# A gated block behind low-rank attention on one core: the gate by x-times-sigmoid, scores in pairs

## The chip, the cores and the metric

One NeuronCore of a Trainium2 chip runs the whole program; the other cores are idle. The metric is the time of one execution on the device in microseconds (us). TensorE (PE) multiplies matrices into PSUM, with its weight loads shown as an engine of their own (PEld). VectorE (DVE) and ScalarE (ACT) can read PSUM, GpSimd (POOL) works on SBUF alone here, and SyncE (SP) issues transfers.

## The reference

Eight batches of eight heads, 1024 positions, 64 columns per head. Keys and values are first projected along the sequence to 64 rows, then ordinary softmax attention is computed over those 64, the heads are put side by side, and a gated feed-forward block follows:

```python
k_proj = einsum('ks,bhsd->bhkd', E, k)
v_proj = einsum('ks,bhsd->bhkd', F, v)
scores = (q @ k_proj.T) / sqrt(64)          # per batch and head
attn   = softmax(scores)                    # over the 64 projected rows
x      = heads side by side(attn @ v_proj)  # 8192 x 512
g      = x @ w_gate                         # 8192 x 1536
silu   = g * (1 / (1 + exp(-g)))
out    = (silu * (x @ w_val)) @ w_out       # 8192 x 512
```

## The kernel before

Tokens are worked in 16 chunks of 512, two to each batch; `c` counts chunks and `c = 2b` is the first of batch `b`. A chunk has 12 tiles `f` of 128 hidden columns, so there are 192 tiles `t`. The main loop runs over `t`, and each tile has this order:

```python
f_g(c, f, i)              # gate: 4 matmuls, then ACT
run_slot(2 * t)
f_v(c, f, i)              # value: 4 matmuls, then DVE
for fn, *a in late.pop(t, ()):
    fn(*a)                # output product of the chunk before, half sums
run_slot(2 * t + 1)
```

The order is written out by hand: nothing reorders it, and each engine takes its own instructions in it. `f_g` computes the gate in a bank of the PSUM pool `gps` (two banks), and ACT writes its hyperbolic tangent of half the value to `th` (L534). `f_v` computes the value in `vps` (two banks); DVE makes `(th + 1) * g` from the PSUM gate (L541) and then half of that times the value, `hT` in bf16 (L546). Together these are x-times-sigmoid times value, as `x * sigmoid(x) = x / 2 * (1 + tanh(x / 2))`.

The output product of a chunk is done during the next one. From the second chunk on it has seven products of half size in place of eight (`f_m`, L624), for two row groups: 14 steps `n` per chunk, placed one or two to a tile, six matmuls each. It needs sums of quarters of `hT` (`h_sum`, L607; on POOL for two of them, on DVE for three). Some steps end in copies by ACT (L641 `xs` at steps 1 and 8, which stand in tiles 1 and 7; L648 `ysb` at steps 3 and 10, in tiles 3 and 9) and in sums by DVE and POOL (L643, L653, L654, L659), and then SP stores the rows.

The attention of batch `b` is spread over the tiles of the batch before it in the loop. `place(b)` writes its units into slots, two slots to a tile, counted from `s0 = 48 * (b - 1)`, which is the first tile of chunk `2b - 2`: `u_KV` projects keys and values, `u_KT` turns the keys, `u_TD` turns the queries by DMA on SP's queue. Eight score units `u_S` have 4 matmuls each (L364) into a bank of the pool `a` (two banks), and ACT takes the exponential (L372) into `ee`. `u_R` makes row sums and reciprocals on DVE (L394, L395), `u_N` scales the weights on POOL (L409) and adds to a watched sum (L425). `u_AD` turns the weights by DMA on SP's queue after four units, `u_PVt` multiplies by the values, and ACT copies the result to `xT` (L477). In the kernel before, the eight score units stand at eight different slots, about three slots apart. Loads of the next batch's keys, values and queries are issued on POOL's queue.

After the loop a branch leads to a general path for scores that need their maximum subtracted; the inputs here do not take it.

Of the kernel before, what the change touches and what calls it, by code (L numbers as in the profile page):

```python
# [9 lines left out]
AF = mybir.ActivationFunctionType  # L10
ALU = mybir.AluOpType
AX = mybir.AxisListType
BF16 = mybir.dt.bfloat16
FP32 = mybir.dt.float32

B = 8
# [6 lines left out]
P = 128  # L23
# [3 lines left out]
NFT = DFF // P  # L27
CH = 2
CW = 512
# [3 lines left out]
HC = DM // 2  # L33
HT = CW // 2
ENG = [getattr(mybir.EngineType, n) for n in ("PE", "DVE", "Activation", "SP", "Pool")]
BY_DMA = [(b, ch) for b in range(1, B) for ch in range(CH)]


@with_exitstack
def kernel(  # L40
# [19 lines left out]
    nc = tc.nc  # L60
    scale = 1.0 / float(D) ** 0.5
# [7 lines left out]
    h_pool = ctx.enter_context(tc.tile_pool(name="hT", bufs=2))  # L69
# [27 lines left out]
    kb, vb, qb, xT, hT = {}, {}, {}, {}, {}  # L97
# [50 lines left out]
    maxed = []  # L148
# [160 lines left out]
    qT, ee, rr, AA, AT = {}, {}, {}, {}, {}  # L309
    by_dma = list(BY_DMA)  # L310

# [195 lines left out]
    gp = {}  # L507
# [3 lines left out]
    def f_mm(c, f, w, i=None):  # L511

        if i != 1:


            where = "y" if (c, f, w) == (0, 2, 0) else "gv"[w]
            half[c, f, w] = bank(where, [P, CW], FP32, where + "ps")
        ps = half[c, f, w]
        x = xT[divmod(c, CH)]
        ts = slice(0, CW) if i is None else slice(256 * i, 256 * (i + 1))  # L520
        for kt in range(NKT):
            nc.tensor.matmul(  # L522
                out=ps[:, ts],
                lhsT=(wg, wv)[w][:, kt, f * P : (f + 1) * P],
                rhs=x[:, kt, ts],
                start=(kt == 0),
                stop=(kt == NKT - 1),
            )
        return ps

    def f_g(c, f, i=None):
        ps = f_mm(c, f, 0, i)
        th = fw.tile([P, CW], FP32, name="th", tag="th")
        nc.scalar.activation(out=th[:], in_=ps[:], func=AF.Tanh, scale=0.5)  # L534
        gp[0] = (ps, th)

    def f_v(c, f, i=None):
        ps = f_mm(c, f, 1, i)
        g, th = gp.pop(0)
        s1 = fw.tile([P, CW], FP32, name="s1", tag="s1")  # L540
        nc.vector.scalar_tensor_tensor(  # L541
            out=s1[:], in0=th[:], scalar=1.0, in1=g[:], op0=ALU.add, op1=ALU.mult
        )
        if f == 0:
            hT[c] = h_pool.tile([P, NFT, CW], BF16, name="hT", tag="hT")
        nc.vector.scalar_tensor_tensor(  # L546
            out=hT[c][:, f, :], in0=s1[:], scalar=0.5, in1=ps[:], op0=ALU.mult, op1=ALU.mult
        )
# [173 lines left out]
    def put(s, fn, *a):  # L722
        slots[s].append((fn, a))

    def place(b):
        s0 = 48 * (b - 1)
        if b == 1:
            put(22, u_TD, 1, 0)
            put(29, u_K1, 1)
            put(32, u_KT, 1)  # L730
            put(40, u_V1, 1)
            sa = (35, 36, 37, 38, 41, 42, 43, 44)
            put(41, u_AD, 1, 0)
            put(30, u_TD, 1, 1)
            put(47, u_AD, 1, 1)
            put(46, u_PVt, 1, 0, (0, 1), ("aa", "av"))
        else:
            if b == 2:
                put(s0 + 10, u_KV, b)
            else:  # L740
                put(s0 + 8, u_KV, b, "kv", (0, H), "v")
            put(s0 + (13 if b == 2 else 11), u_KT, b)
            put(s0 + (9 if b == 2 else -6), u_TD, b, 0)
            put(s0 + (11 if b == 2 else -4), u_TD, b, 1)
            sa = [s0 + j for j in ((17, 18, 22, 23, 27, 30, 33, 36) if b == 2 else (14, 17, 20, 23, 26, 29, 32, 35))]
            put(sa[3] + 4, u_AD, b, 0)
            put(sa[7] + 4, u_AD, b, 1)
            put(s0 + 44, u_PVt, b, 0, (0, 1), ("aa", "yz"))
        for j in range(NJ):
            put(sa[j], u_S, b, j)  # L750
            put(sa[j] + 1, u_R, b, j)
            put(sa[j] + 1, u_N, b, j)
        put(s0 + (68 if b == 1 else 56), u_PVt, b, 1, (0, 1), ("aa", "yz"))

    def run_slot(s):
# [14 lines left out]
    def u_bad():  # L770
        bad.append(nc.values_load(flag[:], min_val=0, max_val=1, skip_runtime_bounds_check_because="is_le gives 0 or 1"))
        tc.mark_branch_hint_location("general", hint=bad[0], engines=tuple(ENG))

    def general():
# [6 lines left out]
        with tc.For_i(0, B) as turn, tc.manual_schedule():  # L781
            turn_of.append(turn)
            b = 0
            load_k(b)
            load_v(b)
            u_KV(b)
            u_KT(b)
            for ch in range(CH):
                c = CH * b + ch
                load_q(b, ch)  # L790
                for u in range(4 * ch, 4 * ch + 4):
                    u_T(b, u)
                    u_S(b, u)
                    u_R(b, u)
                    u_N(b, u)
                    u_A(b, u)
                u_PVt(b, ch, (0, 1), ("aa", "yz"))
                for f in range(NFT):
                    f_g(c, f)
                    f_v(c, f)  # L800
                for m in (1, 2, 5, 6, 7):
                    h_sum(c, m, 0, HF, nc.vector)
                for n in range(14):
                    f_m(c, n)

    with tc.manual_schedule():
# [3 lines left out]
        for i in range(2):  # L810
            nc.scalar.dma_start(
                out=kraw[i][:],
                in_=k[0, 2 * i : 2 * i + 2].rearrange("h (p j) d -> p h (j d)", j=NJ),
# [125 lines left out]
        for b in range(1, B):  # L939
            place(b)  # L940
        for b in range(2, B):
            s0 = 48 * (b - 1) - (20 if b == 3 else 24)
            at = (43, 43, 44, 45) if b == 2 else (s0, s0 + 2, s0 + 4, s0 + 6)
# [31 lines left out]
        for t in range(NIT):  # L975
            c, f = divmod(t, NFT)
            ring["wide"] = c < 2
            i = 1 if t < 2 else None
            f_g(c, f, i)
            run_slot(2 * t)  # L980
            f_v(c, f, i)
            for fn, *a in late.pop(t, ()):
                fn(*a)
            run_slot(2 * t + 1)
# [34 lines left out]
```

## Time and profile before

| | us |
|---|---|
| median of 3 runs | 548.73 |
| lowest and highest | 548.31, 549.86 |
| the profiled execution | 548.89 |
| its span | 547.2 |
| PE busy | 536.7 |
| DVE busy | 413.7 |
| ACT busy | 232.8 |
| POOL busy | 305.9 |

The span runs from the first to the last instruction in the profile. In the rows of a timeline the first number is the start, the second the length of the piece, then engine, line, operation, the written tile and what is read, shapes, the number of instructions merged, and in brackets the idle time before with what ended it. A PE matmul's shown end is modelled and overlaps its successor, so PE's rows are read from start to start.

### The profile page before, as it was taken

How to read it: one execution, taken by the hardware profiler on the slowest of the kernel's cores; microseconds unless marked ns; L12 is line 12 of the kernel's file. 1: busy time of each engine (PE TensorE's matmuls, PEld its weight loads, DVE VectorE, ACT ScalarE, POOL GpSimd, SP SyncE). 2: the span in 40 equal slices, each digit the busy share in tenths (PEclk: the TensorE clock that was granted, in tenths of full speed). 3: DMA queues.
4: the chain of work that ended last, by engine and by line, in shares of the span. 5: the costliest groups of instructions: out<-in, count | busy, mean ns of one | idle time of the engine just before them, and what ended most of it. 6: DMA issues, size and time to landing. Idle time of an engine off the chain costs nothing.

```text
span 547.2 us, 9550 instructions
## 1 busy us (share of the span) xinstructions
PE 536.7 (98%) x3558; PEld 313.6 (57%) x3558; DVE 413.7 (76%) x702; ACT 232.8 (43%) x416; POOL 305.9 (56%) x428
## 2 busy tenths in 40 slices
PE   7999999999999999999999999999999999999996
PEld 3654445556556555566555665566555655555665
DVE  3687897779668876779677795687857887676883
ACT  3565453353444434344434444434444443443331
POOL 6962395478616864177632966248661666416171
PEclk9999999999999999999999999999999999999999
DMA  9999969929921599008961199512991123101003
GB/s 194 191 195 200 159 147 198 173 78 161 196 67 41 103 191 207 21 21 155 197 148 39 40 154 204 106 40 64 184 202 54 39 78 78 40 38 40 8 32 120
DMA packets 112227, 62.92 MB, mean 115 GB/s; under 512 B 65968, under 2 KB 103856, under 8 KB 112176
## 3 DMA queue, kind: packets, MB, share of 16 engines
q0 software_dynamic: 43952, 29.49, 37.6%
q1 hardware_dynamic: 67392, 31.46, 26.3%
q10 hardware_dynamic: 832, 1.31, 0.8%
q8 instruction: 29, 0.48, 0.4%
q14 instruction: 22, 0.18, 0.1%
HBM read 60.29 MB, written 16.78 MB: 141 GB/s over the span
## 4 chain that ended last, share of the span: by engine, by line
PE 94%; DMA 4%; ACT 0%; issue 0%; DVE 0%; POOL 0%; DVEq 0%; ACTq 0%; POOLq 0%
PE vps L522 31%; PE gps L522 30%; PE yps L624 25%; PE sc L364 2%; DMA wv<-in_moe_w_val_dram 2%; PE kvp L173 2%; PE yps L558 2%; PE pv L468 1%; DMA qb<-in_q_dram 1%; POOL AA L409 0%; PE kvp L212 0%; PE kvp L197 0%; PE qTp L329 0%; PE pv L448 0%; PE yps L522 0%
## 5 line engine op out<-in xcount | busy, mean ns | idle before, releaser
L522 PE MATMUL vps<-xT,wv 128*128 128x512 bf16 (+1 forms) x776 | 197.6, 377 | 0.8 <-DMA wv<-in_moe_w_val_dram 0.8
L534 ACT ACTIVATE th<-gps 128x512 f32<-128x512 f32 x191 | 114.1, 597 | 198.3 <-PE gps L522 196.1
L522 PE MATMUL gps<-xT,wg 128*128 128x512 bf16 (+1 forms) x772 | 196.5, 377 | 0.0
L541 DVE SCALAR_TENSOR_TENSOR s<-th,gps 128x512 f32<-128x512 f32 x191 | 129.3, 677 | 60.7 <-ACT th L534 59.5
L546 DVE SCALAR_TENSOR_TENSOR hT<-s,vps 128x512 bf16<-128x512 f32 x192 | 132.1, 688 | 21.7 <-PE vps L522 1.7
L607 POOL TENSOR_TENSOR hs<-hT 128x256 bf16<-128x256 bf16 x180 | 118.9, 683 | 47.2 <-DVE hT L546 46.6
L522 PEld LDWEIGHTS <-wv 128*128 128x128 bf16 x776 | 73.1, 98 | 85.5 <-issue 6.7
L624 PEld LDWEIGHTS <-hs 128*128 128x128 bf16 x900 | 88.1, 98 | 34.6 <-issue 0.6
L522 PEld LDWEIGHTS <-wg 128*128 128x128 bf16 x776 | 74.0, 98 | 51.4 <-issue 0.2
L654 POOL TENSOR_TENSOR tt<-tt,ysb 128x512 f32<-128x512 f32 x28 | 35.6, 1270 | 106.4 <-DVE tt L653 106.4
L409 POOL TENSOR_TENSOR AAd<-ee,zr 128x512 bf16<-128x512 f32 x56 | 58.5, 1044 | 30.1 <-ACT ee L372 17.6
L624 PE MATMUL yps<-ws,hs 128*128 128x256 bf16 x540 | 68.6, 273 | 0.2 <-DVE ysb L693 0.2
L372 ACT ACTIVATE ee<-sc 128x512 f32<-128x512 f32 x64 | 37.8, 595 | 31.6 <-PE sc L364 30.4
L624 PE MATMUL yps<-ws,hT 128*128 128x256 bf16 x360 | 48.8, 273 | 0.0
L624 PE MATMUL yps<-wo,hs 128*128 128x256 bf16 x360 | 48.6, 273 | 0.1
L643 POOL TENSOR_TENSOR tt<-xs 128x256 f32<-128x256 f32 x30 | 28.1, 937 | 36.7 <-ACT xs L641 36.0
L394 DVE TENSOR_REDUCE zr<-ee 128x8 f32<-128x512 f32 x64 | 43.3, 677 | 5.1 <-ACT ee L372 4.8
L607 DVE TENSOR_TENSOR hs<-hT 128x1536 bf16<-128x1536 bf16 (+1 forms) x49 | 45.2, 928 | 0.1
L624 PEld LDWEIGHTS <-hT 128*128 128x128 bf16 x360 | 35.2, 98 | 16.0
L641 ACT COPY xs<-yps 128x512 f32<-128x512 f32 x30 | 17.6, 586 | 28.0 <-PE yps L624 24.7
L648 ACT COPY ysb<-yps 128x512 f32<-128x512 f32 x30 | 17.6, 586 | 27.5 <-PE yps L624 27.5
L477 ACT CAST xT<-pv 128x512 bf16<-128x512 f32 x56 | 28.8, 599 | 0.0
(108 smaller groups left out, 324.0 us busy)
## 6 DMA issues: line engine op xcount, KB each, us to landing
out_dram<-ysb SPq DMA_DIRECT2D x27, 512.0 KB, 2.7
qb<-in_q_dram POOLq DMA_DIRECT2D x14, 512.0 KB, 17.6
kb<-in_k_dram POOLq DMA_DIRECT2D x7, 1024.0 KB, 10.3
vb<-in_v_dram POOLq DMA_DIRECT2D x7, 1024.0 KB, 15.1
wo<-in_moe_w_out_dram POOLq DMA_DIRECT2D x2, 768.0 KB, 21.4
out_dram<-ysb SPq DMA_DIRECT2D x6, 256.0 KB, 2.4
kraw<-in_k_dram ACTq DMA_DIRECT2D x2, 512.0 KB, 4.9
qb<-in_q_dram POOLq DMA_DIRECT2D x4, 256.0 KB, 8.1
```

The source lines that it names most:

```text
L372: nc.scalar.activation(out=e[:].rearrange("p h j k -> p (h j k)"), in_=ps[:].rearrange("p a k -> p (a k)"), func=AF.Exp, scale=scale,)
L394: nc.vector.reduce_sum(out=z, in_=e[:], axis=AX.X)
L409: eng.tensor_tensor(out=a.rearrange("p j h k -> p h j k"), in0=ee.pop((b, u))[:], in1=r.unsqueeze(3).to_broadcast([P, 4, 2, KP]), op=ALU.mult,
L477: nc.scalar.copy(out=xT[b, ch][:, kt, :], in_=ps[:])
L522: nc.tensor.matmul(out=ps[:, ts], lhsT=(wg, wv)[w][:, kt, f * P : (f + 1) * P], rhs=x[:, kt, ts], start=(kt == 0), stop=(kt == NKT - 1),)
L534: nc.scalar.activation(out=th[:], in_=ps[:], func=AF.Tanh, scale=0.5)
L541: nc.vector.scalar_tensor_tensor(out=s1[:], in0=th[:], scalar=1.0, in1=g[:], op0=ALU.add, op1=ALU.mult)
L546: nc.vector.scalar_tensor_tensor(out=hT[c][:, f, :], in0=s1[:], scalar=0.5, in1=ps[:], op0=ALU.mult, op1=ALU.mult)
L607: eng.tensor_tensor(out=hs[c, m][:, fs, :], in0=quarter(hT[c], *a)[:, fs], in1=quarter(hT[c], *b)[:, fs], op=op,)
L624: nc.tensor.matmul(out=ps, lhsT=lhsT, rhs=ws[m][:, f, :] if rhs is None else rhs, start=(start and f == 0), stop=(f == HF - 1), skip_group ...
L643: nc.gpsimd.tensor_tensor(out=t[:, 0], in0=xs[:, 0], in1=xs[:, 1], op=ALU.add)
L654: nc.gpsimd.tensor_tensor(out=t[:], in0=t[:], in1=yo[c, p][:, 1:3], op=ALU.subtract)
```

## The change

From the third chunk on, ACT computes x-times-sigmoid of the gate in one instruction and DVE multiplies it by the value in one step. The tiles in the list `TANGENT` keep the old form: all of chunks 0 and 1 and, for each batch from 2 on, one tile in each of its two groups of score units. The score units of batches 2 to 7 are put in pairs at the ends of two neighbouring tiles, with the tangent tile between the pairs, and their row sums and normalisations follow at one or two slots' distance. The units of batch 1 stay where they were. The transposes of the weights stand at slots 27 and 38.

```diff
+TANGENT = [(c, f) for c in range(CH) for f in range(NFT)] + [
+    x for b in range(2, B) for x in ((2 * b - 2, 9 if b == 2 else 8), (2 * b - 1, 2))
+]
...
     def f_g(c, f, i=None):
         ps = f_mm(c, f, 0, i)
         th = fw.tile([P, CW], FP32, name="th", tag="th")
-        nc.scalar.activation(out=th[:], in_=ps[:], func=AF.Tanh, scale=0.5)
-        gp[0] = (ps, th)
+        if (c, f) in TANGENT and not maxed:
+            nc.scalar.activation(out=th[:], in_=ps[:], func=AF.Tanh, scale=0.5)
+            gp[0] = (ps, th)
+        else:
+            nc.scalar.activation(out=th[:], in_=ps[:], func=AF.Silu)
+            gp[0] = (None, th)
 
     def f_v(c, f, i=None):
         ps = f_mm(c, f, 1, i)
         g, th = gp.pop(0)
+        if f == 0:
+            hT[c] = h_pool.tile([P, NFT, CW], BF16, name="hT", tag="hT")
+        if g is None:
+            nc.vector.tensor_tensor(out=hT[c][:, f, :], in0=th[:], in1=ps[:], op=ALU.mult)
+            return
         s1 = fw.tile([P, CW], FP32, name="s1", tag="s1")
...
-            sa = [s0 + j for j in ((17, 18, 22, 23, 27, 30, 33, 36) if b == 2 else (14, 17, 20, 23, 26, 29, 32, 35))]
-            put(sa[3] + 4, u_AD, b, 0)
-            put(sa[7] + 4, u_AD, b, 1)
+            sa = [s0 + j for j in ((17, 17, 19, 19) if b == 2 else (15, 15, 17, 17)) + (27, 27, 29, 29)]
+            put(s0 + 27, u_AD, b, 0)
+            put(s0 + 38, u_AD, b, 1)
...
         for j in range(NJ):
             put(sa[j], u_S, b, j)
-            put(sa[j] + 1, u_R, b, j)
-            put(sa[j] + 1, u_N, b, j)
+            at = sa[j] + (1 if b == 1 else 1 + j % 4)
+            put(at, u_R, b, j)
+            put(at, u_N, b, j)
```

More of the change, by code (lines that the diff above doesn't have):

```diff
@@ L543, in f_v @@
         )
-        if f == 0:
-            hT[c] = h_pool.tile([P, NFT, CW], BF16, name="hT", tag="hT")
         nc.vector.scalar_tensor_tensor(
```

## The prediction

> **What bounds the kernel now.** I read the page's engine totals first.
>
> ```profile
> PE 536.7 (98%) x3558; PEld 313.6 (57%) x3558; DVE 413.7 (76%) x702; ACT 232.8 (43%) x416; POOL 305.9 (56%) x428
> PE   7999999999999999999999999999999999999996
> PEclk9999999999999999999999999999999999999999
> ```
>
> TensorE (PE) is busy in every slice but the first and the last, at the full granted clock; VectorE (DVE) and ScalarE (ACT), which the change touches, have room. A modelled busy share does not prove that PE runs at its pace, so I read PE's waits next (us in total, times, longest).
>
> ```profile
> PE warm L845 <- DVE zeros L823: 1.4, 1, 1.4
> PE vps L522 <- DMA wv<-in_moe_w_val_dram: 0.8, 1, 0.8
> PE efp L833 <- DMA Eraw<-in_E_dram: 0.8, 1, 0.8
> PE sc L364 <- DVE BD L161: 0.7, 1, 0.7
> ...
> PE yps L624 <- DVE ysb L693: 0.2, 1, 0.2
> ```
>
> All of these lie in the first 22 us except the last, which is at 540.6 us. Then I rebuilt one batch from the timeline. Pitches, start to start: four matmuls of gate or value 0.864 us, six of the output product 0.655, a score unit 0.225, the key/value projection 1.85, its transposes 0.12, a group of four attention products 0.65. One batch has 48 of the first, 28 of the second, 8 score units, one projection and two product groups: 41.47 + 18.34 + 1.80 + 1.85 + 0.12 + 1.30 = 64.88 us. In the chain the projections start at 158.37, 223.23 and 288.08 us, so a batch takes 64.86 us. From the third chunk on (82 us) PE's order has no hole. A cheaper ACT or DVE can therefore buy nothing there; the change can only keep this or open holes. So the question is where PE starts to wait.
>
> These rows price it (start, duration in us).
>
> ```profile
> 237.06 0.39 PE L364 MATMUL sc<-BD,qTd 128*128 128x128 bf16 x4
> 237.28 1.03 PE L522 MATMUL gps<-xT,wg 128*128 128x512 bf16 x4
> 237.48 0.60 ACT L372 ACTIVATE ee<-sc 128x512 f32<-128x512 f32 x1 [1.14 <-PE sc L364]
> ...
> 249.86 0.82 PE L624 MATMUL yps<-ws,hT 128*128 128x256 bf16 x6
> 250.52 1.03 PE L522 MATMUL gps<-xT,wg 128*128 128x512 bf16 x4
> 250.72 0.59 ACT L641 COPY xs<-yps 128x512 f32<-128x512 f32 x1 [0.66 <-PE yps L624]
> ```
>
> A PE group's successor starts when its last column is in; ACT starts 0.20 us after that (237.28 to 237.48, 250.52 to 250.72). The start of the program gives three more prices.
>
> ```profile
> 1.98 1.28 ACT L161 ACT_TABLE_LOAD   x1 [1.98 <-issue]
> 9.69 0.37 ACT L181 CAST ks<-kvp 64x256 bf16<-64x256 f32 x1 [1.13 <-PE kvp L173]
> 10.11 0.29 PE L294 MATMUL kTp<-ident_bf,ks 128*128 128x64 bf16 x4
> 15.56 1.57 ACT L372 ACTIVATE ee<-sc 128x512 f32<-128x512 f32 x3
> ```
>
> One table load takes 1.283 us in the groups by form. PE follows an ACT result after 0.05 us (10.06 to 10.11). Three exponentials in 1.57 us, each 0.595 long, start (1.57 - 0.595)/2 = 0.487 apart, so neighbours overlap by 0.11.
>
> **The change, part by part.** *Gate.* 24 tiles of the first two chunks and 12 later ones keep the tangent; 192 - 36 = 156 tiles take x-times-sigmoid. Each loses one DVE step (L541, 0.677 us), 105.6 us in all, and the other (L546, 0.688) becomes a product of the same operand shapes, which I price at the 0.68 of the final sum of that shape (L659). DVE falls from 413.7 to about 308 us, on the path nothing. ACT still makes one pass per tile; I price it at the tangent's 0.597 (ACT's rows for 512 columns all lie at 0.586 to 0.597); were it twice that, its bank would still be wanted a tile (2.4 us) later. The gate's PSUM bank comes free one DVE step earlier, which nobody waited for.
>
> *Table loads.* Before, exponential and tangent share one table: the trace has a single load. In the changed program's instruction order ACT has 26 loads on the normal path: the old one, one before the first new gate, and two around each of the 12 groups of four score units (two groups in each of batches 2 to 7). 25 x 1.283 = 32 us of ACT, which has 314 us free. The first (about 83 us) sits behind a copy that ends near 83.1; the gate then ends near 85.0, and its bank is wanted again at 87.1: no cost. The load that ends a group delays the next gate to about 6.5 us on the clock used below; PE wants that bank at 9.0: no cost.
>
> *Scores in pairs.* PE's work is the same, moved. The two score banks rotate, so the third unit waits for the first unit's exponential and the fourth for the second's. Clock zero is the end of the tile's last output product. PE: units one and two to 0.45, then gate and value of the tangent tile (1.73), six output products (0.655): the third unit is due at 2.83, the fourth at 3.06. ACT: the output sum's copy (L641) stands ahead of the load in its queue; it starts at 0.20, ends at 0.79. Load to 2.07, first exponential to 2.67, second to 2.07 + 0.487 + 0.595 = 3.15. With 0.05 for the release the third unit could go at 2.72 (in time by 0.11) and the fourth at 3.20: PE stands for 0.15 us. Queued behind it are all of PE's later tiles, so a stall is lost for good. Eleven groups have this shape. In the twelfth (batch 2's first, tiles 8 and 9) no copy precedes the load; it waits for the first unit alone and begins at 0.225 + 0.20 = 0.42, which is 0.37 earlier: no stall.
>
> The unknown is what a load costs at its two edges between other instructions, which no row shows. If it overlapped like two exponentials at each edge (0.11 twice), the stall would be 0.15 - 0.22, that is none. If instead each edge adds a full fixed part of an ACT instruction, it grows: copies of 256 and 512 columns take 0.372 and 0.586, so the fixed part is 0.372 - 0.214 = 0.16, twice is 0.32, and the stall is 0.47. I take the middle, 0.24: 11 x 0.24 = 2.6 us. The ends are 0 and 11 x 0.47 = 5.2; a copy that starts 0.05 late, as some do (234.93 for 234.88), and as much again on the release bring 6.3.
>
> The Trainium skill speaks against such a change: "ScalarE: Activation LUTs", section "What ACT_TABLE_LOAD costs", counts a drain of about 1.38 us on top of a 1.28 us load for every switch, and its rule is to group calls by table set. The trace shows the 1.283 and no second switch. By that page (an estimate) eleven groups would stall 0.15 + 1.38 and the twelfth 0.37 less, together 18 us.
>
> *Softmax tail.* Row sums and normalisations of a pair are put one slot apart or more; the transposes of the weights leave SP's queue at slots 27 and 38 for 27 and 39 or 40. The first pair's last normalisation is queued at slot 21 or 23 against 24, the second's at 33 against 36 or 37, and their readers stand at slots 44 and 56; SP's rows for the transposes last 8.2 and 9.5 us, and 17 slots of 1.35 us lie before the reader: no cost. POOL gets one normalisation more (1.04 + 0.22) into the tiles where it makes the half sums. In the trace their last one ends at 248.71 and PE wants it in the product at 252.24: covered by 3.5 us, and if that were gone every missing us would come on top, per batch.
>
> *Sum.* The profiled execution took 548.89 us, its span 547.2, 1.69 lie around it: 548.9 + 2.6 = 551.5. The median of the runs is 548.73, 0.16 lower, so 551.3.
>
> **Rivals.** *Not slower: the switch fits.* If a load begins under the copy's end and the first exponential under the load's, the fourth unit finds its bank free at 3.06 and nothing changes: 548.7 to 550.3. It decides where the stall is under 0.15 us, which is 1.65 us or 0.3%, about what a measurement of this kernel can tell from no change. For it: other ACT neighbours overlap by 0.11. Against: it needs that overlap at both edges of every load, and only neighbours of one kind show it.
>
> *The switch is far dearer than its row.* After the one load the next ACT instruction starts 4.2 us later, waiting for PE, so the trace can't exclude a hidden tail. At a second load length (1.28) the sum is 11 x 1.43 + 1.06 = 16.8: 565.5. Against: no row shows such a tail.
>
> *DVE's relief makes it faster.* This needs PE to be waiting for DVE; after 22 us it does for 0.2 us in all, so 548.5 and no measurable gain.
>
> *Bunched POOL work or a late transpose reaches PE.* It needs to eat 3.5 us; at 1 us beyond that in each of 6 batches, 555.
>
> **How the numbers follow.** Stall of the forecast's size 0.58; switch fits 0.26; dear switch 0.10; POOL or transpose 0.03; a gain that I can't see 0.03. Slower 0.71, same 0.26, faster 0.03. The range runs from 548.6 (fits) to 555.0 (all edges at their upper bound); the dear switch and a gain stay outside.
>
> **What would show it.** In the changed profile: 26 table loads of 1.283; DVE near 308 us and ACT near 264; PE's waits with a new row, scores on ACT's exponential, 11 or more times at 0.1 to 0.5 us; the batch period up by twice that. Wrong: a period of 64.86 (it fits), a gap beside each load well over 0.3 us (dear switch), PE waiting for half sums or transposed weights, or a period below 64.86.

## The result, and the profile after

The changed kernel takes 552.89 us (median of 5 runs, 552.4 to 553.28), beside 548.68 us for the kernel before on the same chip: 1.0075 times as long, 95% interval 1.006 to 1.009. The forecast was 551.3 in a range of 548.6 to 555.0. The profiled execution has a span of 551.6 us against 547.2.

First the engine totals and the group of the new product, from the page of the changed kernel.

```profile
PE 540.7 (98%) x3558; PEld 314.2 (57%) x3558; DVE 313.6 (57%) x546; ACT 260.1 (47%) x441; POOL 304.3 (55%) x428
...
L550 DVE TENSOR_TENSOR hT<-th,vps 128x512 bf16<-128x512 f32 x156 | 106.4, 682 | 146.8 <-PE vps L525 140.2
```

DVE gave back 100 us (313.6 busy, where it was 413.7) and the kernel became slower: PE was the bound before and is now. The page hardly shows the loss: PE stays at 98%. Next are ScalarE's groups by form, the loads among them (count, busy us, mean ns, idle before).

```profile
L541 ACT ACTIVATE th<-gps 128x512 f32<-128x512 f32 x156 | 93.4, 599 | 192.7 <-PE gps L525 190.6
...
L541 ACT ACT_TABLE_LOAD x13 | 16.7, 1283 | 0.2
L375 ACT ACT_TABLE_LOAD x12 | 15.4, 1283 | 1.3 <-PE sc L367 1.1
```

With the old one that makes 26 loads. Now the timeline of one group of four score units, the first of a batch (start us, length us; PE's rows are read start to start).

```profile
235.69 0.82 PE L634 MATMUL yps<-ws,hT 128*128 128x256 bf16 x6
...
236.34 0.61 PE L367 MATMUL sc<-BD,qTd 128*128 128x128 bf16 x8
236.59 0.59 ACT L651 COPY xs<-yps 128x512 f32<-128x512 f32 x1 [0.93 <-PE yps L634]
...
237.20 1.28 ACT L375 ACT_TABLE_LOAD   x1
...
238.49 1.09 ACT L375 ACTIVATE ee<-sc 128x512 f32<-128x512 f32 x2
...
239.17 0.85 PE L367 MATMUL sc<-BD,qTd 128*128 128x128 bf16 x8
...
239.85 1.03 PE L525 MATMUL gps<-xT,wg 128*128 128x512 bf16 x4
```

The first pair of score units takes 236.34 to 236.79, 0.45 us; the second takes 239.17 to 239.85, 0.68 us. The second exponential ends at 239.58, and the fourth unit starts 0.05 later, at 239.63 instead of 239.395: a stall of 0.235 us. The table load stands between the copy and the exponentials.

PE's waits of the changed kernel do not list this stall, because a matmul's shown end is modelled and covers most of it: four gate matmuls are shown as 1.03 us long, where the next group starts after 0.864, so 0.17 us of idle time can hide there. What they list in the loop is this.

```profile
PE yps L634 <- ACT xT L480: 0.8, 1, 0.8
```

Its place is batch 2's first group.

```profile
108.76 0.61 PE L367 MATMUL sc<-BD,qTd 128*128 128x128 bf16 x8
...
109.21 1.03 PE L525 MATMUL gps<-xT,wg 128*128 128x512 bf16 x4
...
109.61 1.13 ACT L375 ACTIVATE ee<-sc 128x512 f32<-128x512 f32 x2
...
110.30 1.11 PE L471 MATMUL pv<-AT,VS 64*64 64x512 bf16 x8
...
110.76 1.28 ACT L541 ACT_TABLE_LOAD   x1
...
111.34 1.04 PE L525 MATMUL vps<-xT,wv 128*128 128x512 bf16 x4
...
112.55 2.05 ACT L480 CAST xT<-pv 128x512 bf16<-128x512 f32 x4
...
113.18 1.47 PE L634 MATMUL yps<-ws,hs 128*128 128x256 bf16 x12 [0.80 <-ACT xT L480]
```

The score units themselves do not wait here. But batch 1's second value product is put into the next tile and needs the two score banks: it starts 0.13 us late and takes 1.04 us in place of 0.56 (110.25 to 110.81 before), since the second pair's exponentials still hold a bank. Then the attention copies of batch 1 queue behind the exponentials, the load that ends the group, and a gate; the output product, which writes the bank that the first copy empties, starts 0.97 us late. Together 1.6 us. These are the rows of that product before:

```profile
110.25 0.63 PE L468 MATMUL pv<-AT,VS 64*64 64x512 bf16 x8
...
110.81 1.04 PE L522 MATMUL vps<-xT,wv 128*128 128x512 bf16 x4
```

A third, small loss recurs a few tiles behind the second group of each batch, here in DVE's queue.

```profile
195.89 0.67 DVE L397 TENSOR_REDUCE zr<-ee 128x8 f32<-128x512 f32 x1
...
196.72 0.65 DVE L550 TENSOR_TENSOR hT<-th,vps 128x512 bf16<-128x512 f32 x1
...
197.28 0.41 DVE L663 TENSOR_TENSOR tt<-tt,yps 128x256 f32<-128x256 f32 x1
...
197.75 0.82 PE L634 MATMUL yps<-ws,hs 128*128 128x256 bf16 x6
```

A row sum and its tile's product stand ahead of the sum step L663, and the output product that goes on in the same bank starts 0.07 us late, six times.

The account from the starts: 11 x 0.235 = 2.6, batch 2 1.6, six times 0.07 = 0.4, in all 4.6 us. The chain of work that ended last agrees: the projections of successive batches start about 65.39 us apart where they were 64.86 apart, 0.53 more for two stalls of 0.235 and one of 0.07.

```profile
225.12 1.85 PE kvp L176 x16
290.50 1.85 PE kvp L176 x16
```

Up to the loop's projection in the third chunk the changed run is 0.53 us shorter (95.36 against 95.89). All of this is there when the third chunk starts (81.77 against 82.30), and up to there the two kernels do the same. From the start of PE's last matmul to the end the changed run is 0.34 longer; 4.6 - 0.53 + 0.34 = 4.4, which is the difference of the spans.

### The profile page after: what moved, and what is told of

Its sections match the earlier page's. It is cut to its first block, busy times and chain, and to the rows that moved or that the text cites. A ratio compares the mean times of both kernels' runs of the same rounds, so it can differ in the third digit from the quotient of the medians.

```text
span 551.6 us, 9406 instructions
## 1 busy us (share of the span) xinstructions
PE 540.7 (98%) x3558; PEld 314.2 (57%) x3558; DVE 313.6 (57%) x546; ACT 260.1 (47%) x441; POOL 304.3 (55%) x428
## 3 DMA queue, kind: packets, MB, share of 16 engines
q10 hardware_dynamic: 832, 1.31, 0.8%
## 4 chain that ended last, share of the span: by engine, by line
PE 85%; ACT 6%; DMA 3%; POOL 2%; issue 1%; DVE 1%; ACTq 0%; POOLq 0%; DVEq 0%
PE vps L525 27%; PE gps L525 27%; PE yps L634 23%; ACT L375 3%; ACT ee L375 2%; PE kvp L176 2%; PE yps L568 2%; PE sc L367 2%; DMA qb<-in_q_dram 1%; DMA Fraw<-in_F_dram 1%; PE pv L471 1%; POOL wv L139 1%; POOL AA L412 1%; ACT xs L651 0%; POOL wg L139 0%
## 5 line engine op out<-in xcount | busy, mean ns | idle before, releaser
L550 DVE TENSOR_TENSOR hT<-th,vps 128x512 bf16<-128x512 f32 x156 | 106.4, 682 | 146.8 <-PE vps L525 140.2
L653 POOL TENSOR_TENSOR tt<-xs 128x256 f32<-128x256 f32 x30 | 23.4, 781 | 47.2 <-ACT xs L651 46.8
L617 DVE TENSOR_TENSOR hs<-hT 128x1536 bf16<-128x1536 bf16 (+1 forms) x49 | 47.6, 976 | 0.1
L375 ACT ACTIVATE ee<-sc 128x512 f32<-128x512 f32 x64 | 35.6, 606 | 4.3 <-POOL zsum L428 2.5
L556 DVE SCALAR_TENSOR_TENSOR hT<-s,vps 128x512 bf16<-128x512 f32 x36 | 24.8, 688 | 4.2 <-DVE s L553 0.5
```

The costliest lines, as they stand in the source:

```text
L375: nc.scalar.activation(out=e[:].rearrange("p h j k -> p (h j k)"), in_=ps[:].rearrange("p a k -> p (a k)"), func=AF.Exp, scale=scale,)
L550: nc.vector.tensor_tensor(out=hT[c][:, f, :], in0=th[:], in1=ps[:], op=ALU.mult)
L556: nc.vector.scalar_tensor_tensor(out=hT[c][:, f, :], in0=s1[:], scalar=0.5, in1=ps[:], op0=ALU.mult, op1=ALU.mult)
L617: eng.tensor_tensor(out=hs[c, m][:, fs, :], in0=quarter(hT[c], *a)[:, fs], in1=quarter(hT[c], *b)[:, fs], op=op,)
L653: nc.gpsimd.tensor_tensor(out=t[:, 0], in0=xs[:, 0], in1=xs[:, 1], op=ALU.add)
```

## The experiments

The theory: TensorE has no hole, and every loss is a bank that comes free late because a table load, or something behind one, stands in ScalarE's queue ahead of the instruction that frees it. The main rival: the bunching of row sums and normalisations on DVE and POOL costs the time. All eight kernels were timed in five rounds; the first four share runs of the kernel before with a median of 548.07 us, the other four 548.18 us, and each is read against its own.

**Pairs without the gate.** All tiles keep the tangent.

```diff
-TANGENT = [(c, f) for c in range(CH) for f in range(NFT)] + [...]
+TANGENT = [(c, f) for c in range(NC) for f in range(NFT)]
```

> The gate keeps the tangent and its two DVE steps in all tiles; only the placing of the score units, row sums, normalisations and transposes is the changed one. Theory (ScalarE's queue: a table load between the sum's copy and the exponentials keeps the fourth score unit from its bank, and in batch 2 keeps exponentials and attention copies late): without loads the eleven stalls of 0.235 us go, and of batch 2's 1.6 us some 0.4 stays, because the value product still needs the two score banks right after the second pair. 549.1 us (548.5 to 549.8), 1 table load. Rival (the bunching of row sums and normalisations on DVE and POOL costs the time): most of the loss stays, 551.5 us or more, since DVE has even more to do.

Measured: 549.52 us, 1.0026 (1.0017 to 1.0035), 1.45 above the kernel before. The eleven stalls are gone, and of batch 2's 1.6 us 0.42 stays, as expected, so the bulk of the loss is the loads'. But 1.45 is more than the 0.4 expected, and the batch period is 65.06, not 64.86. The rest is the small loss in DVE's queue, grown from 0.07 to 0.21 us with two DVE steps per tile:

```profile
193.62 0.68 DVE L395 TENSOR_REDUCE zr<-ee 128x8 f32<-128x512 f32 x1
...
194.46 0.63 DVE L551 SCALAR_TENSOR_TENSOR s<-th,gps 128x512 f32<-128x512 f32 x1
...
195.19 0.69 DVE L554 SCALAR_TENSOR_TENSOR hT<-s,vps 128x512 bf16<-128x512 f32 x1
...
195.80 0.42 DVE L661 TENSOR_TENSOR tt<-tt,yps 128x256 f32<-128x256 f32 x1
...
196.27 0.81 PE L632 MATMUL yps<-ws,hs 128*128 128x256 bf16 x6
```

So the rival is true in part: with the tangent in every tile the bunching costs six times 0.21, 1.3 us. In the changed kernel six times 0.07 are left of it.

**Gate without the pairs.** The new gate in all tiles from the third chunk on; scores at the old slots, and with them row sums, normalisations and transposes as in the kernel before.

```diff
-TANGENT = [...] + [...]
+TANGENT = [(c, f) for c in range(CH) for f in range(NFT)]
...
-sa = ... ((17, 17, 19, 19) if b == 2 else (15, 15, 17, 17)) + (27, 27, 29, 29)
+sa = ... ((17, 18, 22, 23, 27, 30, 33, 36) if b == 2 else (14, 17, 20, 23, 26, 29, 32, 35))
```

> The new gate from the third chunk on in every tile, but the score units at the old eight slots: 96 table loads for them and one at the start of the third chunk. Theory (ScalarE's queue in the stretch of the scores decides): within the 12 tiles that hold a batch's scores ScalarE has 16 loads of 1.283, 12 gates, 8 exponentials and 4 copies, about 35 us of work for 30 us of TensorE time; two us of slack in the banks cover part, so about 3.5 us are lost in each of six batches: 570 us (560 to 576). Rival (loads fit anywhere in ScalarE's idle half; only the pairing is at fault): about 549.

Measured: 562.25 us, 1.0266 (1.0252 to 1.028), 14.2 above the kernel before. The direction was right and the size at the low end: the period is 66.53, so 1.67 us are lost per batch and not 3.5. PE's waits of this kernel name the queue:

```profile
PE yps L632 <- ACT xs L649: 5.0, 5, 1.0
PE pv L469 <- ACT ee L373: 2.0, 1, 2.0
PE gps L523 <- ACT th L539: 1.5, 5, 0.3
```

The output sum's copy and the gates come late behind loads, and the value product behind batch 2's scores again waits for exponentials. ScalarE is busy for 63% of this span (352.4 us, 43% before), so the 96 loads fit into the span as a whole. In the stretches with scores they did not fit without delay.

**The sum's copy on DVE.**

```diff
-        nc.scalar.copy(out=xs[:], in_=xx[c, p][:])
+        copy(nc.scalar if maxed or c == NC - 1 else nc.vector, xs[:], xx[c, p][:])
```

> As the changed kernel, but the copy of the output sums that stands ahead of the table load in ScalarE's queue is made by VectorE (all but the last chunk's). Theory: the load then begins before the pair's scores end (first groups) or right behind the first score (second groups, 0.42 us after the tile), the second exponential is done by 2.85 us against the 3.06 at which the fourth score unit is due, and the eleven stalls of 0.235 us vanish: 2.6 us less, 550.3 us (549.7 to 551.0). Batch 2's first group keeps its loss. Rival (bunched DVE and POOL work): no gain or worse, 552.9 us or more, as DVE gets 30 more copies.

Measured: 550.81 us, 1.0048 (1.0034 to 1.0062), 2.74 above its kernel before where the change was 4.21 above its own. None of the eleven stalls is left in the starts of PE's rows, which is the point of the run, and the small loss in DVE's queue is gone from its six places too. The time fell by 1.5 us and not 2.6 (the two intervals, 3.3 to 4.9 and 1.9 to 3.4 us, leave about 1 us of doubt). DVE now makes the copy late in other tiles, here behind a half sum that ends at 219.50, and the output product waits for it:

```profile
219.42 0.68 DVE L164 COPY xs<-yps 128x512 f32<-128x512 f32 x1
...
220.16 0.81 PE L634 MATMUL yps<-wo,hs 128*128 128x256 bf16 x6
```

Such products start 0.10 us late seven times, and one 0.24 us late.

**Batch 1's second value product at slot 56.**

```diff
-        put(s0 + (68 if b == 1 else 56), u_PVt, b, 1, (0, 1), ("aa", "yz"))
+        put(s0 + 56, u_PVt, b, 1, (0, 1), ("aa", "yz"))
```

> As the changed kernel, but the second value product of batch 1 stands at slot 56, where the other batches have theirs, instead of 68, right behind batch 2's first group of scores. Theory (the 1.6 us lost at 109 to 113 us come from that product waiting for the score banks, and the output product for its attention copies, which queue behind the exponentials, a load and a gate on ScalarE): 1.6 us less, 551.3 us (550.7 to 551.9), and no TensorE wait on the attention copy. Rival (it is the batch's load traffic or start-up noise): no change, 552.9.

Measured: 561.08 us, 1.0238 (1.0224 to 1.0252). The edit brought a wait of its own, which PE's waits show:

```profile
PE pv L471 <- DMA AT<-AAd: 7.1, 1, 7.1
```

The turned weights of batch 1 were not there yet at slot 56. As a test of the total it failed. The 1.6 us behind batch 2's first group are nevertheless gone in it: between batch 2's and batch 3's projections lie 62.12 us, where the changed kernel has 64.36. Of these 2.24 us, 0.65 is the product itself, which stands ahead of that stretch here, and 1.59 is the loss.

**One more copy ahead of each group.**

```diff
+    def u_X():
+        nc.scalar.copy(out=BDV[:].rearrange("p a d -> p (a d)"), in_=wo[:, 0, :])
...
+            if b > 1 and j % 4 == 0:
+                put(sa[j], u_X)
             put(sa[j], u_S, b, j)
```

> As the changed kernel, with one more ScalarE copy of 512 columns (its result is used by nothing) queued ahead of the table load of each of the twelve groups of scores. Theory: in eleven groups whatever stands ahead of the exponentials adds to TensorE's stall one for one, 0.49 to 0.59 us each, so a stall of 0.72 to 0.82 us in place of 0.235 and 5.4 to 6.5 us more than the changed kernel: about 9.6 to 10.7 us above the kernel before, 558.2 us (557.3 to 559.3). In batch 2's first group the copy runs before the scores and costs nothing. Rival (ScalarE has slack there, the stall is something else): no more than 1 us.

Measured: 558.37 us, 1.0181 (1.0167 to 1.0195), 10.2 above the kernel before; 558.2 was expected. The timeline of the same kind of group:

```profile
240.01 0.82 PE L634 MATMUL yps<-wo,hs 128*128 128x256 bf16 x6
240.51 1.08 ACT L375 ACTIVATE ee<-sc 128x512 f32<-128x512 f32 x2
...
241.16 0.87 PE L367 MATMUL sc<-BD,qTd 128*128 128x128 bf16 x8 [0.33 <-ACT ee L375]
...
241.87 1.03 PE L525 MATMUL gps<-xT,wg 128*128 128x512 bf16 x4
```

The third unit starts 1.15 us after the output products in place of 0.655, 0.49 late, and the second pair takes 0.71, 0.26 too long: 0.75 us of stall in place of 0.235. The copy, 0.59 us long and 0.11 of it overlapped by its neighbour, is paid almost whole: what is put ahead of the exponentials adds to the stall.

**No tangent between the pairs.** `TANGENT` as in the second experiment, scores in pairs.

> As the changed kernel, but the tile between the two pairs of a group takes the new gate too, so that a group has four table loads in place of two. Theory, by the same clock: the pair's exponentials end at 3.24 us, a load at 4.5, the gate at 5.1, a load at 6.4, the second pair's exponentials at 7.5, a load at 8.8, the next gate at 9.4, and TensorE wants that gate's bank at 8.94: 0.4 to 0.5 us of new stall in eleven groups, and 2 to 3 us in batch 2's first group, where the value product waits for the second pair. 4.7 + 2.7 = 7.4 us more than the changed kernel, 11.6 above the kernel before, 559.7 us (558 to 562). Rival (two more loads fit in ScalarE's idle half): no change from the changed kernel.

Measured: 575.38 us, 1.049 (1.0475 to 1.0504), 27 above the kernel before, where 11.6 was expected. PE's waits:

```profile
PE yps L632 <- DVE tt L661: 11.4, 11, 1.4
PE gps L523 <- ACT th L539: 4.6, 11, 0.4
```

The second row is the stall that was expected, 0.57 to 0.59 us of lost start in each of eleven groups. The first was not. The gate behind the second pair comes late on ScalarE, behind the pair's exponentials and a load, and DVE's product of that gate waits for it. Behind that product DVE's queue holds a row sum and another product, and only then the sum step of the output, for which PE waits:

```profile
187.82 0.69 DVE L548 TENSOR_TENSOR hT<-th,vps 128x512 bf16<-128x512 f32 x1 [2.78 <-ACT th L539]
...
189.83 0.41 DVE L661 TENSOR_TENSOR tt<-tt,yps 128x256 f32<-128x256 f32 x1
...
190.29 0.82 PE L632 MATMUL yps<-ws,hs 128*128 128x256 bf16 x6 [0.56 <-DVE tt L661]
```

PE loses 0.73 us behind the first group of batches 3 to 7 and 1.60 behind every batch's second. It is the small third loss of the changed kernel, grown large. In batch 2's first group the same queues cost about 6.2 us, of which the value product's wait for exponentials is the largest (2.9 in PE's waits). The losses in the starts of this profile add up to 28 us: 11 x 0.235, 11 x 0.58, 5 x 0.73, 6 x 1.60 and 6.2.

**Batch 2's first group two slots earlier.**

```diff
-    x for b in range(2, B) for x in ((2 * b - 2, 9 if b == 2 else 8), (2 * b - 1, 2))
+    x for b in range(2, B) for x in ((2 * b - 2, 8), (2 * b - 1, 2))
...
-sa = ... ((17, 17, 19, 19) if b == 2 else (15, 15, 17, 17)) + (27, 27, 29, 29)
+sa = ... (15, 15, 17, 17) + (27, 27, 29, 29)
```

> As the changed kernel, but batch 2's first group of scores stands two slots earlier, where the other batches have theirs (slots 15 and 17, tangent in tile 8), so that two tiles lie between it and batch 1's value product. Theory: the 1.6 us at that product vanish, and the group gets the common stall of 0.235 instead: 1.35 us less than the changed kernel, 2.85 above the kernel before, about 551.2 us (550.5 to 552.0). Rival (it is the batch itself, not the neighbour on ScalarE's queue): no change. If the turned queries are not there at slot 15, TensorE waits for that transfer instead, and the trace says so.

Measured: 551.28 us, 1.0053 (1.0039 to 1.0066), 3.1 above the kernel before; 551.2 was expected. The wait on the attention copies is gone, and the stall in the group is 0.18 us; its sum copy starts 0.20 us after the output products, where those of the eleven start 0.25 after.

**Both mended.** The last edit, and the copy on DVE in the twelve tiles that lead to a group.

```diff
+        copy(nc.vector if 1 <= c < NC - 3 and c % 2 == p and not maxed else nc.scalar, xs[:], xx[c, p][:])
```

> Both mended: batch 2's first group two slots earlier, and the copy of the output sums ahead of the twelve groups made by VectorE (in those twelve tiles alone). Theory: no stall is left on ScalarE's queue, the batch period is 64.86 to 64.95, and the time is that of the kernel before within 0.6 us, 548.6 us; it can't be less, as TensorE had no hole before. Rival: whatever remains above the kernel before by more than 1 us is a cost of the new gate, the pairs or the loads that the theory does not know.

Measured: 548.29 us beside 548.18, 1.0000 (0.9991 to 1.0009). A group in its timeline, and the projections in its chain:

```profile
233.12 1.28 ACT L375 ACT_TABLE_LOAD   x1
...
233.78 0.61 PE L367 MATMUL sc<-BD,qTd 128*128 128x128 bf16 x8
234.00 0.68 DVE L164 COPY xs<-yps 128x512 f32<-128x512 f32 x1
...
234.42 1.09 ACT L375 ACTIVATE ee<-sc 128x512 f32<-128x512 f32 x2
...
236.61 0.61 PE L367 MATMUL sc<-BD,qTd 128*128 128x128 bf16 x8
...
237.05 1.03 PE L525 MATMUL gps<-xT,wg 128*128 128x512 bf16 x4
```

```profile
222.55 1.85 PE kvp L176 x16
287.41 1.85 PE kvp L176 x16
```

In this group the load starts 0.66 us ahead of the scores, the exponentials follow right behind it, the second pair takes 0.44 us, and the period is 64.86 again. That early start is seen in five of the twelve groups. In the other seven ScalarE is idle, yet the load waits for the first score unit and starts 0.47 us after it (here the unit starts at 103.40):

```profile
103.87 1.28 ACT L375 ACT_TABLE_LOAD   x1 [1.19 <-PE sc L367]
```

That is early enough as well: no stall is left in the starts of PE's rows. The same 26 loads are there and cost nothing. The third loss has vanished too, with nothing done to it but the earlier exponentials and the earlier tangent gate behind them. No version was faster than the kernel before.

## Why the prediction was right, and where it was off

*PE is the bound and has no hole, so DVE's relief buys nothing: right.* The last experiment settles it: 93 us less of DVE (320.4 for 413.7) and a period that equals the old one to 0.01 us. The totals came near the forecast, DVE at 313.6 for 308 and ScalarE at 260.1 for 264, and neither bears on the time.

*Eleven stalls at the fourth score unit: right in the mechanism, and in the size partly by luck.* Forecast 0.24, measured 0.235 in each; 2.6 us of the sum. Its parts were other than thought: 0.15 from the clock, 0.05 because the copy starts 0.25 and not 0.20 us after the output products, and 0.035 for the load's two edges, where 0.09 had been taken. The group of the seventh experiment whose copy starts at 0.20 stalls 0.18. The load begins 0.02 us after the copy ends and the exponential 0.01 after the load, so the edges lose the overlap of neighbours and add next to nothing. The upper bound, a fixed part at each edge, was far too high, and the middle was right because the late copy filled it. The late start could have been read beforehand: of the 28 sum copies in the loop of the kernel before, 15 start about 0.26 us after the products and 13 start 0.20 after, and the row that the forecast used is one of the 13.

*The twelfth group has no stall: true of the score units, wrong of the group.* This is the step that failed: the forecast was 2.6 us and the loss 4.2, and 1.6 of it is here. The working followed the score banks and the gates but not the next user of those banks and the next work in ScalarE's queue, batch 1's value product in the tile behind. It cost 1.6 us; moving the group by two slots took that away (3.1 above the kernel before in place of 4.2, with the group's own small stall added).

*Softmax tail at no cost: nearly right.* POOL and the transposes cost nothing in the trace. DVE's queue was not walked: row sums stand ahead of the sum step L663, 0.4 us in all. The step was priced by each unit's reader, not by what is queued behind it.

*The rivals.* That the switch fits fell by 0.235 us a group, and came true once the copy and batch 2's group were moved. The dear switch fell: copy end to exponential start is 1.31 us (237.18 to 238.49), so the drain of 1.38 us that the Trainium skill adds to each load ("ScalarE: Activation LUTs", section "What ACT_TABLE_LOAD costs") does not show here, and its 18 us were not lost; the load of 1.283 is as the page has it. Its rule to group calls by table set (section "Table sets: the hidden batching unit") is borne out in part: 96 loads of ungrouped calls cost 14.2 us and the 26 of the last experiment nothing, but 50 in badly placed groups cost 27, so here the place decided more than the number. Of the rival of bunched work, the transposes and POOL's half sums did not reach PE; it was DVE's row sums that did, by 0.4 us.

*What would show it.* PE's period and the loads came as written; the new row in PE's waits did not, since the stall hides under the modelled ends. It had to be read from starts; the row appears in the fifth experiment, where the stall is longer (scores on ScalarE's exponential, 3.6 us in 11 waits).

## What to carry to other kernels

On a kernel whose bound engine has no hole, a saving elsewhere bought nothing here, and an edit is priced by walking each in-order queue that it lengthens: what stands ahead of the instruction that frees a bank, and who takes that bank next, in the neighbouring stage too. In these runs a table load was free where nothing late stood ahead of it in ScalarE's queue and nothing that others wait for stood right behind it: moving a 0.59 us copy off the queue ahead of each group, and one group by two slots, made all the loads of this kernel free. Short stalls are read from start to start, not from the list of waits.

## What the runs showed of the hardware that was not expected

A table load between two ScalarE instructions took 1.283 us with edges of 0.01 to 0.02 us. In the last experiment it ran ahead of the scores in five of twelve groups (233.12, the scores at 233.78), right behind the gate before it. In the other seven it waited for the first score unit after 1.19 us of idle time. No run shows what decides between the two. More than half of the output sums' copies on ScalarE start 0.25 to 0.26 us after the last product and the others 0.20 after; the cause was not tested.
